# One-pass transposed scores with wide exponentials, V stationary in PV, and the FFN woven into attention

## The chip, the cores and the metric

The kernel runs on one core of one Trainium2 chip. The metric is device time in microseconds (us) of one execution; the profile is one such execution taken by the hardware profiler.

Names used below: PE is the tensor engine, DVE the vector engine, ACT the scalar engine, POOL the GpSimd engine. "Granted clock" is the share of full speed that the chip let PE run at.

## The reference, cut to what matters

Two layers, each an attention block and a gated FFN with the same weights in both layers. S = 2048 rows, D = 512, 32 heads of 16, F = 1792.

```python
for _ in range(2):
    h = layernorm(x)
    q, k, v = split(h @ wqkv)                        # 32 heads of width 16
    p = softmax(q @ k.T * 16 ** -0.5)                # 2048 x 2048 for each head
    x = x + (p @ v) @ wo
    h = layernorm(x)
    x = x + (gelu(h @ w_gate) * (h @ w_up)) @ w_down
```

The softmax is what costs: 32 heads x 2048 x 2048 = 134 million exponentials per layer, or 1024 tiles of 128x1024.

## The kernel before

Work is cut into units of 4 heads and 512 queries, 32 units a layer. Each unit is worked through twice, 32 steps each time. Pass 1 computes scores with queries on the partitions and finds each row's maximum on DVE. The maxima are folded into a shifted copy of Q. Pass 2 computes the scores again, transposed (keys on the partitions), takes the exponential on ACT in tiles of 128x512, and multiplies with V. In that product the exponentials are the stationary operand and V, with a column of ones for the row sums, streams 17 columns wide. The FFN follows when attention is finished.

```python
# pass 1, one step: two heads' scores, and their row maxima on DVE
for jj in range(2):
    j = 2 * hp + jj
    ins = e.matmul(bank(2 * buf + jj),
                   lhsT=QT1[32 * j:32 * j + 32, s, qt * 128:(qt + 1) * 128],
                   rhs=KT[32 * j:32 * j + 32, g, kb * 512:(kb + 1) * 512],
                   start=True, stop=True, tile_position=(32 * j, 0))
...
sch.op("dve", lambda e, po=po, buf=buf: e.tensor_reduce(po, PS[:, 2 * buf:2 * buf + 2, :], axis=AX.X, op=ALU.max), ...)
# pass 2, one step: two heads' transposed scores, two exponentials of 512 columns
for jj in range(2):
    ...
    sch.op("pe", lambda e, ...: e.matmul(bank(bk), lhsT=KT[...], rhs=QT2[...], ..., tile_position=(32 * j, 0)), ...)
    sch.op("act", lambda e, bk=bk, slot=slot: e.activation(PT[:, slot, :], bank(bk), ACTF.Exp, scale=DH ** -0.5), ...)
# PV: exponentials stationary, V and the ones column moving
for qt in range(4):
    acc = AP(PS, 7 * 512 + (qt * 4 + j) * 17, [[8 * 512, 128], [1, 17]])
    ins = e.matmul(acc, lhsT=PT[:, slot, qt * 128:(qt + 1) * 128], rhs=VP[:, kt, 4 * g + j, :], ...)
# filler: zero weights, in steps with little other work for PE
for i in range(n_mm):                      # n_mm = 3
    ins = e.matmul(PS[:, 7, NACC:512], lhsT=ZER[:, :], rhs=XNT[:, 0, 0:512 - NACC], start=False, stop=False, ...)
```

## Time and profile before

| | before |
|---|---|
| median | 2828.22 us (3 runs, 2822.28 to 2829.49) |
| busy: PE, DVE, ACT | 2626.5, 2504.3, 2470.2 us of a span of 2824.1 |
| mean granted PE clock | 0.994 |

The groups of instructions, costliest first (`...` stands for lines left out). Columns: line, engine, operation, output and inputs, shapes, count; busy us and mean ns of one; idle time of that engine just before them, and what ended it.

```profile
L775 DVE TENSOR_REDUCE PM<-PS 128x2 f32<-128x1024 f32 x2048 | 2335.3, 1219 | 42.5 <-PE PS L797 27.2
L801 ACT ACTIVATE SCR<-PS 128x512 bf16<-128x512 f32 x4096 | 2187.0, 598 | 57.3 <-PE PS L797 0.8
...
L737 PE MATMUL PS<-XNT,ZER 128*128 128x240 bf16 x5562 | 869.5, 264 | 22.9 <-ACT ACCS L647 22.9
...
L819 PE MATMUL PS<-VP,SCR 128*128 128x17 bf16 x16384 | 729.2, 172 | 0.0
```

The row maxima (L775) fill 2335 us with 43 us of idle time before them: DVE sets the pace, at 2335.3 / 2048 = 1.14 us per step. ACT is close behind, 2187.0 / 4096 = 0.534 us per exponential, two per step. L737 is the filler.

The chain of waits, followed back from the last instruction, says the same:

```profile
DVE 76%; PE 15%; ACT 6%; DMA 1%; POOL 1%; issue 1%; ACTq 0%; DVEq 0%; POOLq 0%
```

Stretches of the span: busy us of PE, weight loads, DVE, ACT and POOL, then the granted PE clock. The first is attention of layer 1, the second part of its FFN.

```profile
70.00:1200.00 1130.00, 1053.08 (x14700) 541.66 (x14699) 1116.05 (x1011) 1089.78 (x2074) 120.92 (x72) 1.00 0.01 2
1270.00:1340.00 70.00, 69.13 (x554) 51.58 (x552) 31.62 (x75) 29.07 (x70) 17.75 (x26) 1.00 0.01 1
```

In the FFN stretch ACT is 42% busy (29.07 of 70). The two FFN phases, from the last exponential (1261 and 2662 us) to the next row maximum (1429) or the end (2824), take about 165 us each, and no exponential runs in them.

### The profile page before, as it was taken

How to read it: one execution, taken by the hardware profiler on the slowest of the kernel's cores; microseconds unless marked ns; L12 is line 12 of the kernel's file. 1: busy time of each engine (PE TensorE's matmuls, PEld its weight loads, DVE VectorE, ACT ScalarE, POOL GpSimd, SP SyncE). 2: the span in 40 equal slices, each digit the busy share in tenths (PEclk: the TensorE clock that was granted, in tenths of full speed). 3: DMA queues.
4: the chain of work that ended last, by engine and by line, in shares of the span. 5: the costliest groups of instructions: out<-in, count | busy, mean ns of one | idle time of the engine just before them, and what ended most of it. 6: DMA issues, size and time to landing. Idle time of an engine off the chain costs nothing.

```text
span 2824.1 us, 75969 instructions
## 1 busy us (share of the span) xinstructions
PE 2626.5 (93%) x33850; PEld 1411.6 (50%) x33850; DVE 2504.3 (89%) x2500; ACT 2470.2 (87%) x4742; POOL 353.4 (13%) x315
## 2 busy tenths in 40 slices
PE   6999999999999999999989999999999999999999
PEld 2444444444444444457734444444444444444576
DVE  6899999999999999934478999999999999999243
ACT  4899999999999999994339999999999999999832
POOL 3000010001000110012200000100010001000210
PEclk9999999999999999999999999999999999999999
DMA  5000000000000000000000000000000000000000
GB/s 168 1 2 2 2 2 2 2 2 2 2 2 2 2 2 2 2 2 1 1 1 2 2 2 2 2 2 2 2 2 2 2 2 2 2 2 2 2 16 16
DMA packets 9721, 18.75 MB, mean 7 GB/s; under 512 B 433, under 2 KB 6321, under 8 KB 9393
## 3 DMA queue, kind: packets, MB, share of 16 engines
q1 hardware_dynamic: 7280, 9.70, 1.1%
q8 instruction: 265, 4.34, 0.6%
q0 software_dynamic: 2112, 4.19, 0.4%
q14 instruction: 64, 0.52, 0.1%
HBM read 9.70 MB, written 2.10 MB: 4 GB/s over the span
## 4 chain that ended last, share of the span: by engine, by line
DVE 76%; PE 15%; ACT 6%; DMA 1%; POOL 1%; issue 1%; ACTq 0%; DVEq 0%; POOLq 0%
DVE PM L775 73%; PE PS L366 6%; ACT SCR L801 3%; PE PS L430 2%; DVE HT L497 2%; PE PS L766 2%; ACT FSC L490 2%; PE PS L458 1%; PE PS L819 1%; PE PS L681 1%; PE PS L737 1%; DMA X<-in_A_x_dram 1%; PE PS L797 1%; DVE ST L315 1%; ACT AO L687 0%
## 5 line engine op out<-in xcount | busy, mean ns | idle before, releaser
L775 DVE TENSOR_REDUCE PM<-PS 128x2 f32<-128x1024 f32 x2048 | 2335.3, 1219 | 42.5 <-PE PS L797 27.2
L801 ACT ACTIVATE SCR<-PS 128x512 bf16<-128x512 f32 x4096 | 2187.0, 598 | 57.3 <-PE PS L797 0.8
L766 PE MATMUL PS<-KT,SCR 32*128 32x512 bf16 x4096 | 797.0, 386 | 128.8 <-DVE PM L775 1.2
L797 PE MATMUL PS<-QT,KT 32*128 32x512 bf16 x4096 | 889.0, 385 | 4.2 <-ACT SCR L801 1.6
L737 PE MATMUL PS<-XNT,ZER 128*128 128x240 bf16 x5562 | 869.5, 264 | 22.9 <-ACT ACCS L647 22.9
L819 PEld LDWEIGHTS PS<-VP,SCR 128*128 128x128 bf16 x16384 | 547.5, 96 | 435.7 <-issue 434.9
L819 PE MATMUL PS<-VP,SCR 128*128 128x17 bf16 x16384 | 729.2, 172 | 0.0
L766 PEld LDWEIGHTS PS<-KT,SCR 32*128 32x128 bf16 x4096 | 192.3, 91 | 644.7 <-DVE PM L775 566.0
L650 POOL TENSOR_TENSOR RL<-ACCS,CM 128x16 f32<-128x16 f32 x64 | 185.9, 2905 | 2111.4 <-ACT ACCS L647 2111.4
L737 PEld LDWEIGHTS PS<-XNT,ZER 128*128 128x128 bf16 x5562 | 401.0, 96 | 66.7 <-ACT ACCS L647 41.1
L797 PEld LDWEIGHTS PS<-QT,KT 32*128 32x128 bf16 x4096 | 247.7, 90 | 59.5 <-ACT SCR L801 36.9
L490 ACT ACTIVATE FSC<-PS 128x256 bf16<-128x256 f32 x224 | 85.2, 383 | 161.4 <-DVE HT L497 88.0
L497 DVE TENSOR_TENSOR HT<-PS,FSC 128x256 bf16<-128x256 f32 x224 | 92.8, 422 | 136.4 <-ACT FSC L490 123.9
L366 PE MATMUL PS<-FSC,WG 128*128 128x256 bf16 x896 | 135.2, 274 | 0.4 <-ACT FSC L490 0.4
L366 PE MATMUL PS<-FSC,WU 128*128 128x256 bf16 x896 | 134.9, 273 | 0.0
L366 PE MATMUL PS<-WD,HT 128*128 128x512 bf16 x448 | 99.6, 379 | 3.9 <-DVE HT L497 3.7
L366 PEld LDWEIGHTS PS<-FSC,WG 128*128 128x128 bf16 x896 | 87.8, 98 | 15.3 <-ACT FSC L490 0.7
L436 ACT ACTIVATE KT<-PS,KBIAS 128x512 bf16<-128x512 f32 x64 | 44.0, 687 | 58.5 <-PE PS L430 58.5
L366 PEld LDWEIGHTS PS<-FSC,WU 128*128 128x128 bf16 x896 | 87.5, 98 | 10.3
L430 PE MATMUL PS<-XNT,WKP 128*128 128x512 bf16 x256 | 72.1, 408 | 5.6 <-ACT XNT L350 3.1
L366 PEld LDWEIGHTS PS<-WD,HT 128*128 128x128 bf16 x448 | 42.8, 98 | 55.1 <-issue 3.4
L607 PE MATMUL PS<-XNT,WQP 128*128 128x512 bf16 x248 | 63.5, 377 | 0.0
(58 smaller groups left out, 732.7 us busy)
## 6 DMA issues: line engine op xcount, KB each, us to landing
X<-in_A_x_dram POOLq DMA_DIRECT2D x4, 1024.0 KB, 15.1
out_dram<-OB SPq DMA_DIRECT2D x16, 128.0 KB, 1.7
WG<-in_B_w_gate_dram SPq DMA_DIRECT2D x1, 1792.0 KB, 19.7
WU<-in_B_w_up_dram SPq DMA_DIRECT2D x1, 1792.0 KB, 25.4
WD<-in_B_w_down_dram SPq DMA_DIRECT2D x1, 1792.0 KB, 28.6
SCR<-in_A_wqkv_dram SPq DMA_DIRECT2D x2, 512.0 KB, 4.4
WV<-in_A_wqkv_dram SPq DMA_DIRECT2D x1, 512.0 KB, 9.3
WO<-in_A_wo_dram SPq DMA_DIRECT2D x1, 512.0 KB, 13.0
```

The source lines that it names most:

```text
L366: ins = e.matmul(out_ap, lhsT=l, rhs=r_, start=(i == 0), stop=(i == n - 1 and extra is None))
L430: ins = e.matmul(bank(bk), lhsT=WKP[:, ck, g, :], rhs=XNT[:, ck, 512 * b:512 * (b + 1)], start=(ck == 0), stop=(ck == n - 1))
L490: sch.op("act", lambda e, bg=bg, gs=gs: e.activation(GT[:, gs, :], bank(bg)[:, 0:256], ACTF.Gelu_apprx_tanh), r=[BK[bg]], w=[("GT", gs)])
L497: sch.op("dve", lambda e, bu=bu, gs=gs, ft=ft: e.tensor_tensor(ht(ft), bank(bu)[:, 0:256], GT[:, gs, :], op=ALU.mult), r=[BK[bu], ("GT", g ...
L607: ins = e.matmul(bank(bk), lhsT=WQP[:, ck, g, :], rhs=XNT[:, ck, 512 * qb:512 * (qb + 1)], start=(ck == 0), stop=(ck == n - 1))
L650: sch.op("pool", lambda e: e.tensor_tensor(RL[:, s, :], lsum, CM1[:, :], op=ALU.pow), r=[("ACCS", s), ("CM1",)], w=[("RL", s)])
L737: ins = e.matmul(PS[:, 7, NACC:512], lhsT=ZER[:, :], rhs=XNT[:, 0, 0:512 - NACC], start=False, stop=False, skip_group_check=True)
L766: ins = e.matmul(bank(2 * buf + jj), lhsT=QT1[32 * j:32 * j + 32, s, qt * 128:(qt + 1) * 128], rhs=KT[32 * j:32 * j + 32, g, kb * 512:(kb ...
L775: sch.op("dve", lambda e, po=po, buf=buf: e.tensor_reduce(po, PS[:, 2 * buf:2 * buf + 2, :], axis=AX.X, op=ALU.max), r=[BK[2 * buf], BK[2 ...
L797: sch.op("pe", lambda e, bk=bk, j=j, kt=kt, s=s, g=g: e.matmul(bank(bk), lhsT=KT[32 * j:32 * j + 32, g, kt * 128:(kt + 1) * 128], rhs=QT2[ ...
L801: sch.op("act", lambda e, bk=bk, slot=slot: e.activation(PT[:, slot, :], bank(bk), ACTF.Exp, scale=DH ** -0.5), r=[BK[bk]], w=[("PT", slot)])
L819: ins = e.matmul(acc, lhsT=PT[:, slot, qt * 128:(qt + 1) * 128], rhs=VP[:, kt, 4 * g + j, :], start=(st and qt == 0), stop=False, skip_gro ...
```

## The change

Intent: drop the first pass. The scores are small enough here to take the exponential without a row maximum, so DVE's 2335 us, the second score matmul and the shift of Q go. Scores are computed once, transposed. One exponential covers two banks, 128x1024. In PV, V with its ones column becomes the stationary operand (17 columns), four heads side by side in four column tiles, and the exponentials stream; the row sums come out as row 16 of each tile, and are inverted and spread over 16 partitions through DRAM. With the PE time so freed, projections, layer norm and FFN are woven into attention, through one PSUM bank (bank 6; banks 0 to 5 hold three score slots, bank 7 PV). Only the FFN's gate part does not go through bank 6: its seven pieces per query block take the score slots, one after another in one burst. The filler goes. At the end every engine reads a flag, which says whether the row sums and variances stayed in range; if not, the old two-pass program runs. With these inputs it does not.

The core of it (cut: the old program is kept as the general path; the set-up, the normalisation and the scheduler are left out):

```diff
-    e.tensor_reduce(po, PS[:, 2 * buf:2 * buf + 2, :], axis=AX.X, op=ALU.max)      # DVE, each step
-    e.activation(PT[:, slot, :], bank(bk), ACTF.Exp, scale=DH ** -0.5)             # 512 columns, twice a step
-    e.matmul(acc, lhsT=PT[:, slot, qt * 128:(qt + 1) * 128], rhs=VP[:, kt, 4 * g + j, :], ...)
-    e.matmul(PS[:, 7, NACC:512], lhsT=ZER[:, :], rhs=XNT[:, 0, 0:512 - NACC], ...) # filler
+    def a_slot(layer, u, kt, hp):                    # one step; next_slot() cycles through 3
+        for jj in range(2):
+            j = 2 * hp + jj
+            ins = e.matmul(bank(2 * s + jj), lhsT=KT[32 * j:32 * j + 32, c, kt * 128:(kt + 1) * 128],
+                           rhs=Q[32 * j:32 * j + 32, qs, :], start=True, stop=True, tile_position=(32 * j, 0))
+        sch.op("act", lambda e: e.activation(PT[:, p, :].rearrange("p (a b) -> p a b", a=2), PS[:, 2 * s:2 * s + 2, :],
+                                             ACTF.Exp, scale=SCALE), ...)
+    def pv(layer, u, kt):                            # every second step
+        for j in range(4):
+            ins = e.matmul(PS[32 * j:32 * j + VW, 7, :], lhsT=VP[:, kt, h, :],
+                           rhs=PT[:, ps[j // 2], (j % 2) * 512:(j % 2 + 1) * 512],
+                           start=(kt == 0), stop=(kt == NKT - 1), tile_position=(0, 32 * j), ...)
+    misc = Ring([6])                                 # the one bank for everything else
+    while nxt < len(seqs) or pend:                   # the loop over steps
+        ...
+            a_slot(layer, u, kt, hp)
+            run_pv(step)
+        while spent < BUDGET:                        # 520 ns: K, Q, V projections
+            c = prep_try()
+            ...
+        while spent < BUDGET and posts:              # output projection, layer norm, FFN
+            c = next(posts[0], "end")
+            ...
```

An item of four 512-column matmuls is counted as 864 ns, so one such item fills a step's budget. In this text "item" means one piece of this other work, "step" one `a_slot`, and "turn" a step in which items may run. An item's "eviction" is the DVE instruction that reads its finished result out of the PSUM bank.

## The prediction

> **What bounds it now.** In attention (70-1260 and 1430-2660 us of the span) VectorE finds row maxima. The cost groups show 2048 reductions of 128x1024 scores, 1219 ns each, 2335 us busy together (1140 ns per step when back to back), with 43 us of idle time before them. The chain of waits gives DVE 76%, that reduction alone 73%. ScalarE follows closely: 4096 exponentials of 128x512, 598 ns each, 2187 us busy. The FFN stands apart: in the stretches table, 1270-1410 and 2700-2824 us, ACT falls to about a third busy; about 175 us per layer.
>
> **What the change does.**
> - Row maxima (2335 us DVE), the second score matmul, the shift of Q and the 5562 filler matmuls go. DVE falls to about 400 us: projections' evictions and adds (128x512, 692 ns each) and layer norm.
> - Exp works on 128x1024. Read from the trace: 598 ns at 512 columns, 383 (gelu) at 256, so 0.84 ns per column; in a row 8 instructions took 4.48 us, the last counted whole, so about 545 ns apart. At 1024 columns I estimate 0.97 us step to step: 2048 x 0.97 = 1985 us. 56 gelus add 55 us, about 14 more table loads (1283 ns) 15 us. ScalarE is the new floor: about 2055 us.
> - Scores, PE: two row-tiled matmuls per step. The trace has four of them in 0.42 us, so they run concurrently. PV becomes four column tiles of 17x512 every second step; no run before shows these. The Trainium skill ("TensorE: Matmul & The Clock Gate", Measured speedup vs the span model) gives three column tiles 2.38x, so I take about 0.3 us plus about 0.15 us drain per mode change ("TensorEngine Tiling (Array Packing)", Key Properties; the trace shows about 0.15 us between the scores' streaming and PV). Two steps need about 1.1-1.3 us of PE against 1.94 us of ACT: attention alone is ACT-bound.
> - FFN, projections and layer norm are spread through attention, through ONE PSUM bank. A four-matmul group streams 0.86 us, then about 0.28 us to the reader's start, 0.69 us DVE, about 0.07 us release: about 1.9 us per such item, and PE is in order, so the scores of the next step wait. Such a step costs 1.9 instead of 0.97 us; three PSUM slots hide only two steps. Per query block: 14 up items +12 us, down +9, four output projections of eight matmuls +7, transposes +4, gate burst (7 x 1.73 us PE) +4. About 36 us x 6 blocks = 215, and 56 K/V items + 50: about 265 us.
>
> **What stays exposed.** Start: 42 us (as before: X arrives by 29 us, then all four transposes). Layer boundary: layer 1's first unit needs the last block's FFN after 24 steps: about 50 us. End: DMA normalisation 13, output projection 8, layer norm and transposes 7, gate 12, up 12, down 13, store and branch 5: about 70 us.
>
> **Sum:** 2055 + 265 + 42 + 50 + 70 = 2480 us, 12% less. Range 2370 to 2620. Faster by over 2%: 0.92; within 2%: 0.05; slower: 0.03.
>
> **What would show it.** ACT about 2050 us busy (above 80%), DVE below 20%; exp about 1.03 us each; in stretches without projections ACT fully busy, in stretches with them exp waiting for score matmuls, and matmuls of the miscellaneous group waiting for DVE evictions; a boundary hole of about 50 us near the middle; four PV matmuls starting within a few ns of each other.
>
> **What would make it wrong.** Column tiles running one after another (about 1.1 us per PV): PE would bind everywhere, near 2800. Evictions overlapping better, or slack absorbing the bursts: near 2300. Normalisation's small DMAs stalling DVE or GpSimd, then PE: slower.

## The result, and the profile after

| | before | after |
|---|---|---|
| median | 2828.85 us (4 runs) | 2505.85 us (4 runs, 2504.71 to 2512.08) |
| ratio | | 0.8855 (95% interval 0.8817 to 0.8893) |
| busy: PE, DVE, ACT | 2626.5, 2504.3, 2470.2 us | 2159.2, 361.0, 1993.2 us |
| mean granted PE clock | 0.994 | 0.659 |

Ratios here and below are those for the runs of the same rounds, so not quite the ratio of the medians quoted beside them. Every kernel below was timed beside the kernel before, whose median stayed between 2824.8 and 2828.9 us; the variants are compared with one another by their medians.

The groups after:

```profile
L613 ACT ACTIVATE fPT<-fPS 128x1024 bf16<-128x1024 f32 x2048 | 1913.4, 1184 | 390.8 <-PE fPS L608 389.3
L608 PE MATMUL fPS<-fQ,fKT 32*128 32x512 bf16 x4096 | 1102.1, 553 | 172.5 <-ACT fPT L613 163.4
L626 PE MATMUL fPS<-fPT,fVP 128*17 128x512 bf16 x4096 | 573.1, 550 | 1.4 <-ACT fPT L613 1.4
...
L323 PE MATMUL fPS<-fXNT,fWU 128*128 128x512 bf16 x448 | 111.6, 381 | 23.2 <-DVE fHT L513 18.1
```

The exponentials are the largest group, and ACT waited 389 us for score matmuls before them. (The mean duration of 1184 ns is longer than the time from one to the next, because exponentials in a row overlap: 2048 of them keep ACT busy for 1913.4 us only. One that starts on an idle ACT takes 1.02 us.) Score and PV matmuls take 550 ns, an up projection's 381 ns. That difference is the clock: by the 40 slices of the span, in tenths,

```profile
ACT  1689976999769996899727899679986899769971
...
PEclk7855569555795558756588655785568655695558
```

PE runs at about half speed for most of the time in which attention runs alone (from 458 to 500 us the granted clock was 0.50 throughout), and the slices inside attention where ACT drops to 6 or 7 are mostly those where the clock is up, that is, where items run.

The chain of waits is now mostly exponentials:

```profile
ACT 54%; PE 31%; DVE 8%; DMA 3%; POOL 2%; SPq 2%; issue 1%; POOLq 0%; DVEq 0%
```

The timeline of attention alone. Columns: start us, duration, engine, line, operation, and in brackets the idle time before it and its releaser. In this and the next timelines the rows of weight loads, and of engines and operations that the text does not speak of, are left out.

```profile
599.46 9.32 ACT L613 ACTIVATE fPT<-fPS 128x1024 bf16<-128x1024 f32 x10
599.67 0.60 PE L608 MATMUL fPS<-fQ,fKT 32*128 32x512 bf16 x2 [0.53 <-ACT fPT L613]
600.20 0.61 PE L626 MATMUL fPS<-fPT,fVP 128*17 128x512 bf16 x4
600.74 0.60 PE L608 MATMUL fPS<-fQ,fKT 32*128 32x512 bf16 x2
601.50 0.61 PE L608 MATMUL fPS<-fQ,fKT 32*128 32x512 bf16 x2 [0.15 <-ACT fPT L613]
```

Ten exponentials run without a gap. Elsewhere 32 of them take 29.44 us; with the last counted whole (1.02 us) that is (29.44 - 1.02) / 31 = 0.917 us per step. PE waits for ACT, not the reverse. Four PV matmuls together take 0.61 us, as long as two score matmuls, so the column tiles run side by side.

The same view where up projections run:

```profile
400.50 0.39 PE L608 MATMUL fPS<-fQ,fKT 32*128 32x512 bf16 x2
400.60 0.69 DVE L513 TENSOR_TENSOR fHT<-fPS,fHT 128x512 bf16<-128x512 f32 x1 [1.13 <-PE fPS L323]
400.81 0.39 PE L626 MATMUL fPS<-fPT,fVP 128*17 128x512 bf16 x4
400.93 1.02 ACT L613 ACTIVATE fPT<-fPS 128x1024 bf16<-128x1024 f32 x1 [0.80 <-PE fPS L608]
401.35 1.04 PE L323 MATMUL fPS<-fXNT,fWU 128*128 128x512 bf16 x4
402.32 0.39 PE L608 MATMUL fPS<-fQ,fKT 32*128 32x512 bf16 x2
...
402.75 1.02 ACT L613 ACTIVATE fPT<-fPS 128x1024 bf16<-128x1024 f32 x1 [0.80 <-PE fPS L608]
```

A step takes 402.75 - 400.93 = 1.82 us, twice as long, and ACT idles 0.80 us in it. The eviction (L513) of one item ends at 401.29 and the next item starts at 401.35: the single bank is the loop. PE is at full clock here (0.39 instead of 0.61 us).

A single Q projection inside attention, at half clock:

```profile
239.21 1.89 PE L323 MATMUL fPS<-fXNT,fWQM 128*128 128x512 bf16 x4
241.03 0.61 PE L608 MATMUL fPS<-fQ,fKT 32*128 32x512 bf16 x4
241.68 1.94 ACT L613 ACTIVATE fPT<-fPS 128x1024 bf16<-128x1024 f32 x2 [0.85 <-PE fPS L608]
```

The four matmuls take 1.89 us instead of 1.04, and ACT idles 0.85 us. There is one in nearly every unit.

### The profile page after: what moved, and what is told of

Same layout as the page of the kernel before. It is cut to its first block, busy times and chain, and to the rows that moved or that the text cites. A ratio compares the mean times of both kernels' runs of the same rounds, so it can differ in the third digit from the quotient of the medians.

```text
span 2504.6 us, 25781 instructions
## 1 busy us (share of the span) xinstructions
PE 2159.2 (86%) x10945; PEld 537.1 (21%) x10945; DVE 361.0 (14%) x634; ACT 1993.2 (80%) x2121; POOL 160.9 (6%) x192
## 4 chain that ended last, share of the span: by engine, by line
ACT 54%; PE 31%; DVE 8%; DMA 3%; POOL 2%; SPq 2%; issue 1%; POOLq 0%; DVEq 0%
ACT fPT L613 54%; PE fPS L323 13%; PE fPS L577 4%; PE fPS L521 4%; PE fPS L608 4%; DVE fHT L513 2%; PE fPS L626 2%; SPq L239 2%; PE fPS L353 2%; DMA fRB<-rscr 1%; PE fPS L308 1%; POOL fXN L295 1%; POOL fAT L437 1%; DVE fVP L358 1%; DVE fKT L343 1%
## 5 line engine op out<-in xcount | busy, mean ns | idle before, releaser
L613 ACT ACTIVATE fPT<-fPS 128x1024 bf16<-128x1024 f32 x2048 | 1913.4, 1184 | 390.8 <-PE fPS L608 389.3
L608 PE MATMUL fPS<-fQ,fKT 32*128 32x512 bf16 x4096 | 1102.1, 553 | 172.5 <-ACT fPT L613 163.4
L626 PE MATMUL fPS<-fPT,fVP 128*17 128x512 bf16 x4096 | 573.1, 550 | 1.4 <-ACT fPT L613 1.4
L608 PEld LDWEIGHTS fPS<-fQ,fKT 32*128 32x128 bf16 x4096 | 198.7, 97 | 1064.0 <-ACT fPT L613 984.9
L437 POOL TENSOR_TENSOR fAT<-fOS,fRB 128x512 bf16<-128x512 f32 x64 | 81.0, 1265 | 1874.9 <-DMA fRB<-rscr 1874.9
L626 PEld LDWEIGHTS fPS<-fPT,fVP 128*17 128x17 bf16 x4096 | 101.1, 90 | 400.0 <-issue 395.8
L323 PE MATMUL fPS<-fXNT,fWU 128*128 128x512 bf16 x448 | 111.6, 381 | 23.2 <-DVE fHT L513 18.1
L521 PE MATMUL fPS<-fWD,fHT 128*128 128x512 bf16 x448 | 113.7, 381 | 13.1 <-DVE fXN L532 4.7
L323 PE MATMUL fPS<-fXNT,fWQM 128*128 128x512 bf16 x256 | 111.8, 587 | 4.3 <-DVE fX L537 1.4
L577 PE MATMUL fPS<-fXNT,fWG 128*128 128x512 bf16 x448 | 110.4, 412 | 0.8 <-DVE fXNT L312 0.5
L513 DVE TENSOR_TENSOR fHT<-fPS,fHT 128x512 bf16<-128x512 f32 x112 | 77.5, 692 | 216.5 <-PE fPS L323 216.3
```

What stands on the lines that cost most here:

```text
L323: ins = e.matmul(bank(b)[:, 0:cols], lhsT=l, rhs=r_, start=(i == 0), stop=(i == n - 1))
L437: sch.op("pool", lambda e, g=g, slot=slot, os_=os_: e.tensor_tensor(AT[:, g, :], OS[:, os_, :], RB[:, slot, :], op=ALU.mult), r=[("OS", os ...
L513: lambda b, ft=ft: sch.op("dve", lambda e: e.tensor_tensor(HT[:, ft, :], bank(b), HT[:, ft, :], op=ALU.mult), r=[BK[b], ("HT", ft)], w=[(" ...
L521: ins = e.matmul(bank(b)[:, 0:D], lhsT=HT[:, ft, i * 128:(i + 1) * 128], rhs=WD[:, ft, :], start=(ft == 0), stop=(ft == NFT - 1))
L577: ins = e.matmul(bank(2 * s + jj), lhsT=WG[:, ck, ft * 128:(ft + 1) * 128], rhs=XNT[:, ck, xs], start=(ck == 0), stop=(ck == NCK - 1))
L608: ins = e.matmul(bank(2 * s + jj), lhsT=KT[32 * j:32 * j + 32, c, kt * 128:(kt + 1) * 128], rhs=Q[32 * j:32 * j + 32, qs, :], start=True, ...
```

## The experiments

Eleven kernels were built from the changed one and run; all gave correct results. A trace of each is compared with those above.

### 1. Two narrow exponentials instead of a wide one

```diff
-        sch.op("act", lambda e: e.activation(PT[:, p, :].rearrange(...), PS[:, 2 * s:2 * s + 2, :], ACTF.Exp, scale=SCALE), ...)
+        for jj in range(2):
+            sch.op("act", lambda e, jj=jj: e.activation(PT[:, p, jj * 512:(jj + 1) * 512], bank(2 * s + jj),
+                                                 ACTF.Exp, scale=SCALE), r=[bks[jj]], w=[("PT", p)])
```

> Two exponentials of 128x512 in place of one of 128x1024, nothing else. Theory A (ScalarE sets the pace in the attention stretches; the wide instruction is what lowered it): 0.918 us per step (29 in 26.68 us in the trace of the changed kernel) becomes 2 x 0.534 = 1.07 us (the kernel before: 2187 us busy over 4096). About 1700 of 2048 steps are paced by ScalarE, so +0.15 x 1700 = about +255 us, near 2760 us. Rival B (TensorE at its half clock, 0.61 us per matmul group, sets the pace of 0.918 and ScalarE only follows): less than +100 us.

Measured: 2805.92 us, ratio to before 0.992 (0.9886 to 0.9953), 300 us slower than the changed kernel (about 255 expected). From the timeline of attention alone:

```profile
599.61 30.75 ACT L614 ACTIVATE fPT<-fPS 128x512 bf16<-128x512 f32 x55
```

55 instructions in 30.75 us are 0.56 us each, 1.12 per step against 0.917. The expectation had 1.07, from the kernel before. Theory A holds. The run also says something plain about the change: with everything else in place but the old exponentials, it was within 2% of the kernel before. By these steps, removing the row maxima alone would only have moved the limit from DVE (1.14 us per step) to ACT (1.12); a kernel with nothing but that removed was not run.

### 2 and 3. The one bank for everything else

Bank 6 can only be joined by others if the score slots give theirs up. So there are two runs: two score slots with two banks idle (the control), and two score slots with banks 4, 5 and 6 for the items.

```diff
-        s = slot_no["n"] % 3
+        s = slot_no["n"] % 2          # both runs
-    misc = Ring([6])                  # and the two later assignments of its banks
+    misc = Ring([4, 5, 6])            # second run only
```

> Score slots cut from three to two, two PSUM banks left unused: the control for the next run. Theory A: only the slack for bursts is lost, about 1 us per burst and per Q projection: +20 to +90 us (2525 to 2600). If the half TensorE clock (score matmuls to the exponential's start about 0.65 us, PV ahead of it another 0.54 us) cannot refill a slot within one exponential of 0.918 us, attention itself slows and it is over +150 us.

> Two score slots, and three PSUM banks instead of one for projections, FFN and transposes. Theory C (the single bank is what makes an up-projection step 1.82 us: matmuls to DVE start 1.07, eviction 0.69, release 0.06): against the two-slot control, up steps fall from 1.82 to about 1.45 us (TensorE alone, as in the down steps, 1.29 without PV and 1.61 with), transposes from 1.12 to about 0.6: 40 to 90 us faster than the control. Rival D (TensorE's own work in the step is the limit): within 15 us of the control.

Measured: control 2584.56 us, with three banks 2477.44 us. The lost slot cost 79 us, as expected, and the two banks gave 107 us against the control, more than the 40 to 90 expected. Exponentials beside up projections in the run with three banks:

```profile
398.71 1.02 ACT L613 ACTIVATE fPT<-fPS 128x1024 bf16<-128x1024 f32 x1 [0.27 <-PE fPS L608]
400.33 1.02 ACT L613 ACTIVATE fPT<-fPS 128x1024 bf16<-128x1024 f32 x1 [0.59 <-PE fPS L608]
401.62 1.02 ACT L613 ACTIVATE fPT<-fPS 128x1024 bf16<-128x1024 f32 x1 [0.27 <-PE fPS L608]
```

Steps now alternate between 1.62 and 1.29 us, with and without PV, in place of 1.82, which the control still shows. Theory C holds: the bank's round trip set 1.82 us. What is left, 1.45 us on average against 0.917, is PE's own work: it is busy for 30.58 of the 31 us from 398 to 429.

### 4. Items in every second step only

```diff
+        turn = step % 2 == 1 or nxt >= len(seqs)
-        while spent < BUDGET:
+        while turn and spent < BUDGET:
             c = prep_try()
...
-        while spent < BUDGET and posts:
+        while turn and spent < BUDGET and posts:
```

> Projections, FFN and transposes only in every second step, those without PV. Theory E (the excess arises because the items come in bursts, step after step, in steps already carrying scores and PV; ScalarE idles 0.9 us per item): two steps with one four-matmul item need about 2.0 us of TensorE (0.32 + 0.97 + 0.32 + 0.32, and drains) against 1.84 us of ScalarE, so an item costs about 0.2 instead of 0.9 us: 100 to 150 us faster, 2355 to 2405. Rival F (the total TensorE work binds over the whole of attention, so moving it changes nothing): within 30 us of 2506.

Measured: 2305.82 us, 200 us faster, more than the 100 to 150 expected. Exponentials beside the up projections and the first downs:

```profile
360.73 35.68 ACT L613 ACTIVATE fPT<-fPS 128x1024 bf16<-128x1024 f32 x38
```

38 in 35.68 us is (35.68 - 1.02) / 37 = 0.937 us per step; ACT does not wait at all. Theory E holds and rival F falls. The miss is in the cost of an item: 2 x (0.937 - 0.917) = 0.04 us, where 0.2 had been estimated. ACT's waiting before exponentials went from 389 to 182 us.

The edit does two things at once: only half of the steps may take items, and none of these steps has PV. No run separates the two.

Not all of the waiting went. The K and V projections at the start of layer 2 still left ACT idle 1.33 us per pair of steps, in this stretch (columns as in the stretches before):

```profile
1190.00:1217.00 27.00, 26.44 (x142) 10.53 (x140) 5.65 (x9) 16.34 (x16) 0.00 (x0) 0.50 0.01 2
```

PE is busy 26.44 of 27 us there, at clock 0.50.

### 5 to 8. The clock, and the FFN taken out again

A filler like that of the kernel before (two matmuls of 512 columns instead of three of 240) was put back, right after PV, in steps without items; once as full-array matmuls and once as column tiles like PV's. It was also combined with spreading. A fourth kernel moved layer norm and FFN of the first three query blocks of each layer behind attention.

```diff
+        if state["fill"] and spent == 0 and nxt < len(seqs):     # state["fill"]: PV ran in this step, not a unit's last
+            def pe_fill(e):
+                for _ in range(2):
+                    ins = e.matmul(bank(7), lhsT=ZER[:, :], rhs=WV[:, 0, :], start=False, stop=False, ...)
```

In the column-tile form the matmul is replaced by this:

```diff
+                    for j in range(4):
+                        ins = e.matmul(PS[32 * j:32 * j + VW, 7, :], lhsT=ZER[:, 0:VW], rhs=WV[:, 0, :],
+                                       start=False, stop=False, tile_position=(0, 32 * j), ...)
```

> Two full-array filler matmuls (zero weights, 512 columns, added to the PV bank) after PV in steps that have no other work, as the kernel before had them. Theory H (the clock is granted by how much of the array works; row-tiled scores and 17-column PV tiles alone leave it at half, 0.50 in the stretches without FFN): mean clock rises from 0.66 to over 0.9; attention stays at 0.918 us per step because ScalarE paces it; but single Q projections (1.89 us at half clock, ScalarE idle 0.9), the first projections of a burst and the transposes (1.12 us each) get short: 60 to 110 us faster than 2506. Rival I (the clock costs nothing because ScalarE paces attention and bursts warm the array themselves): within 20 us, or slower by the fillers.

Measured: 2436.45 us, 69 us faster than the changed kernel, mean clock 0.970. Attention alone did not get faster at full clock:

```profile
788.95 92.58 ACT L615 ACTIVATE fPT<-fPS 128x1024 bf16<-128x1024 f32 x100
```

That is (92.58 - 1.02) / 99 = 0.925 us per step, against 0.917 at half clock. It also runs over three Q projections without a gap; each cost 0.85 us before. ACT's waiting before exponentials fell from 389 to 325 us, nearly all of the gain. So the half clock costs nothing where ACT sets the pace, and 69 us at the items. Theory H was right about the size and about where it lies.

> The same two fillers in the shape of PV, four column tiles of 17 columns each, so the same TensorE time but about an eighth to a half of the array. Theory H: the clock stays near 0.5 in attention although TensorE is busy all the time; at half clock the two fillers need 2 x 0.43 us, so two steps take about 2.5 instead of 1.84 us: about 2900 us or more. If TensorE's busy time alone decided the clock, this run looks like the run with full-array fillers.

Measured: 2435.29 us (two runs), clock 0.970, the same as with full-array fillers. The expectation failed: 17 columns in each column tile kept the clock as well as 128 columns did, so the part of theory H that says how much of the array must work falls.

> Fillers and the spreading over every second step together. In the run with spreading the K and V projections still leave ScalarE idle 1.33 us per two steps, in a stretch whose clock is 0.50, and Q projections 0.5 us each; at full clock both should vanish: 40 to 90 us faster than the spread run, 2215 to 2265. If the clock does not matter once the items are spread: within 20 us of 2306.

Measured: 2375.15 us, 69 us slower than spreading alone. Neither expectation was met. Exponentials beside up projections:

```profile
657.84 1.02 ACT L615 ACTIVATE fPT<-fPS 128x1024 bf16<-128x1024 f32 x1 [0.27 <-PE fPS L610]
659.02 1.02 ACT L615 ACTIVATE fPT<-fPS 128x1024 bf16<-128x1024 f32 x1 [0.16 <-PE fPS L610]
660.31 1.02 ACT L615 ACTIVATE fPT<-fPS 128x1024 bf16<-128x1024 f32 x1 [0.27 <-PE fPS L610]
```

Two steps take 660.31 - 657.84 = 2.47 us. The kernel was badly built: items run in odd steps and PV in even ones, so the test "no item in this step" let the fillers run in the very stretches where PE had no time to spare.

> The FFN of the first three query blocks of a layer taken out of attention and run with the fourth block's at the layer's end, ScalarE idle; output projections stay in attention. In the changed kernel one block's stretch (344.3 to 442.1 us) holds 52 exponentials, 48 us at 0.918, so the block costs 50 us although it is overlapped; about 41 of them are layer norm and FFN. Run apart they take 57 us in layer 1 and 49 in layer 2 by the boundary's and the end's times. Theory J (overlapping earned almost nothing, the excess gives it back): +40 to +90 us, 2545 to 2595. Rival K (overlapping hides most of the FFN): +200 us or more.

Measured: 2608.04 us, 102 us slower than the changed kernel, just above theory J's range and far below rival K's. So weaving six of the eight FFNs into attention earned about 17 us each in this kernel. Run apart, one takes far longer: in this run the FFNs at the end of layer 2 follow each other every 48 us (the first gelus start at 2420.57, 2468.37 and 2516.13 us), those of layer 1 every 68 us, with eight exponentials in between.

### 9 to 11. Putting it together

First, the badly built combination mended: fillers only while no item ran in the last turn.

```diff
+        if turn:
+            state["worked"] = spent
-        if state["fill"] and spent == 0 and nxt < len(seqs):
+        if state["fill"] and state.get("worked", 0) == 0 and nxt < len(seqs):
```

> Spreading as before, fillers only while no projection, FFN or transpose runs (in the run with both, fillers also ran beside every item, because the items are in the steps without PV and the fillers in those with PV; its trace shows 4 pieces of about 2.47 us per two steps there in place of 1.87). Theory L (the fillers beside the items are what made that run slower than spreading alone): the loss goes and Q projections (ScalarE idle 0.5 to 0.9 us each, 58 of them) gain: 2250 to 2295, 10 to 55 us faster than spreading alone (2306). If it stays near 2375 the fillers hurt for another reason.

Measured: 2228.47 us, ratio to before 0.7875, 77 us faster than spreading alone and more than expected. Theory L holds: the fillers beside the items had been the loss.

Then the output projection of eight matmuls was cut into two pieces of four, with the piece boundary handled as in the down projection:

```diff
-            yield out_proj(qb, qt)
+            for g0 in range(0, NG, 4):
+                ...                                   # four matmuls into the same bank
+                if g0 + 4 < NG:
+                    state["open"] = True
+                    yield 864.0
```

> The same with each output projection of eight matmuls cut into two pieces of four in two different turns. Theory E (what matters is that no pair of steps gets more TensorE work than ScalarE covers): the idle times of 1.1 to 3.3 us before the exponentials at the four output projections of each block fall to about 0.2: 10 to 30 us faster than the run before it. Rival: no change, since the first of them waits for the normalisation's DMA anyway.

Measured: 2203.96 us (2195.74 to 2210.19), ratio to before 0.7784 (0.7753 to 0.7816), 24 us faster than the run before it, as expected. This is the fastest kernel, 22% below the kernel before and 12% below the changed one. Its ACT is 90% busy:

```profile
998.52 80.36 ACT L631 ACTIVATE fPT<-fPS 128x1024 bf16<-128x1024 f32 x86
```

ACT waits only 112 us before exponentials, 49 of them at the start.

Last, three banks and two slots with spreading (the edits of runs 3 and 4 together, no filler):

> Spreading with two score slots and three banks for the other work. In the kernel without spreading, the two more banks gave 107 us against the two-slot control. Theory M (with one item every second step its eviction of 0.69 us is over before the next item, so the bank no longer limits; only the lost slot shows): 0 to 60 us slower than spreading alone, 2306 to 2365. If the single bank still limited: over 20 us faster than 2306.

Measured: 2346.31 us, 40 us slower than spreading alone, inside theory M's range: once the items are spread, the third slot is worth more than the two banks. That the single bank then costs nothing at all is not shown by this run, since spreading with two slots and one bank was not run; that ACT did not wait beside the up projections in experiment 4 speaks for it.

## Why the prediction was right or wrong

The time was right: 2480 us predicted, 2506 measured, inside the range. Part of that is luck, since two terms too high (exponentials and gelus, by 123 us) and four too low (by 146 us) nearly cancelled. "Measured" below is the profiled run of the changed kernel, span 2504.6 us.

| term of the sum | predicted | measured | how it was measured |
|---|---|---|---|
| exponentials | 1985 | 1878 | 2048 x 0.917 us per step |
| gelus and their tables | 70 | 54 | 42 gelus before the boundary's and the end's, x 0.917, and 12 table loads x 1.283; the others lie in the holes below |
| start | 42 | 53 | the first exponential starts at 52.74 |
| layer boundary | 50 | 72 | hole from 1231.1 to 1306.2, less 3 exponentials |
| end | 70 | 82 | from 2422.7 to the end |
| excess of the items | 265 | 366 | the rest of the span |

- **What bounds it.** Right. ACT was named as the new floor, and the split run confirms it: 0.2 us more per step cost 300 us. The size was not: the step was over-estimated, 0.97 instead of 0.917 us. The estimate took a spacing of 545 ns from eight exponentials in 4.48 us, and added columns at 0.84 ns. Measured, the 512 added columns cost 0.917 - 0.545 = 0.372 us, 0.73 ns per column: the cost per column was too high.
- **Column tiles side by side.** Right. Four PV matmuls of 512 columns take 0.39 us at full clock, as long as the two score matmuls. The 2.38x for three tiles that the prediction took from the Trainium skill ("TensorE: Matmul & The Clock Gate", "Measured speedup vs the span model") is not tested here, as no run has three.
- **The single bank.** Right. An up step was put at 1.9 us and took 1.82; the reason, the eviction's round trip, was shown by the run with three banks.
- **The filler.** This is the step that failed. The prediction said that "the 5562 filler matmuls go" and counted that as work removed, at no cost; all its item costs were taken at full clock. The granted clock fell from 0.994 to 0.659. The items that come singly or first in a burst then ran at half speed: a Q projection took 1.89 us and left ACT idle 0.85 us, where the prediction charged Q nothing. Putting fillers back gained 69 us, about two thirds of the 101 us by which the excess was under-estimated. The waits of 0.85 us behind single Q projections alone make 40 us: the trace of the changed kernel has 47 of them, that of the kernel with full-array fillers none. The rest of those 101 us was not separated.
- **The holes.** Boundary and end were each too low, by 22 and 12 us. At the end, the normalisation through DRAM took from 2422.7 to 2441.5, 19 us, where 13 had been allowed.
- **What would show it.** ACT was expected at about 2050 us, above 80%: it was 1993, 79.6%. DVE below 20%: 14%. A hole near the middle: seen.
- **What would make it wrong.** None of the three happened to any size: column tiles did not run one after another, the slack did not absorb the bursts, and the normalisation's DMAs cost PE about 2 us per block before the output projection (it waits there for POOL's last product), and at the end 6 us more than allowed.

Where did the gain come from? DVE's 2335 us and the apart FFN's 330 us had left, but ACT was already at 0.534 us per half step, so the maxima alone would have been worth little (argued from the split run). The wide exponential brought about 300 us, and six of the eight FFNs in attention 102; each was measured by taking it alone out of the changed kernel, so they need not add up to the 323 us gained. The rest of the FFN's time was given back as ACT idle time beside bursts, and experiment 4 took 200 us of it back by changing only in which steps the items are issued.

Open: what releases the clock once it has dropped. In two kernels with nearly the same code the K and V projections at the start of layer 2 began at half clock with PE busy all the time; in the run with mended fillers the clock was back within 4 us, in the fastest kernel it stayed at 0.50 for 27 us (first and second line; columns as in the stretches before):

```profile
1159.00:1163.00 4.00, 4.00 (x32) 2.12 (x30) 0.69 (x1) 2.47 (x3) 0.00 (x0) 0.59 0.01 4
1144.00:1171.00 27.00, 27.00 (x144) 10.52 (x142) 5.54 (x8) 16.37 (x16) 0.00 (x0) 0.50 0.00 1
```

No experiment told these apart, and the code need not be the reason. In the one trace of the changed kernel, two single Q projections began alike at half clock, at 531.88 and 622.74 us, each 1.89 us long and followed on PE by scores and PV alone. After the first, score groups took 0.39 us from 534.71 until past 537; after the second they stayed at 0.60. What releases the clock may thus differ from one time to the next, and the four runs of the fastest kernel (2195.74 to 2210.19 us, clock 0.969 to 0.977) fit that.

## What to carry to other kernels

When one engine's long work is removed, look at once at the engine right behind it: here nearly all of the gain was lost again when only ACT's wide instructions were split. Work that is woven in beside a paced engine should be dosed so that no short stretch asks more of PE than the paced engine covers; the same items in every second step were worth 200 us. And before removing filler matmuls, ask which later matmuls rely on the clock that they hold up.

## What the Trainium skill lacked or had wrong

- "TensorE: Matmul & The Clock Gate", Part 1, "What's actually happening": its table gives full clock after at least one busy window of about 3.4 us, and half clock after an idle one. Here attention alone sat at 0.50 with no PE gap above 0.53 us in the timeline shown (from 458 to 500 us PE was busy 38.88 of 42 us, as the profile counts it), and in the run with spreading a stretch with PE busy 26.44 of 27 us stayed at 0.50. The table's two levels do agree: steady stretches show 0.50 or 1.00.
- The same page, "Why this matters for your kernels", advises to avoid idle gaps above about 3 us. That was not enough here; two fillers of 512 columns every second step were (clock 0.66 to 0.97), whether they used 128 columns of the array or 17 in each of four column tiles. No page that was read says what share of the time PE has to be busy to keep the clock.
- The same page, Part 3, "Measured speedup vs the span model", has three column tiles. Four tiles of 17 columns took 0.39 us together, where one full-array matmul of 512 columns has a mean of 0.38.
- "TensorEngine Tiling (Array Packing)", Key Properties, says that a change of tiling mode drains the array but not for how long. Here a score group followed by PV started PV 0.31 us after it at full clock and 0.53 at half; the streaming of 512 columns is 0.22 and 0.43 us of that (estimates: in the kernel before, 28 matmuls of 512 columns in a row took 6.20 us and the last one 0.38 of it, so (6.20 - 0.38) / 27 = 0.216 each, and twice that at half clock). About 0.1 us is left for the drain, less than the 0.15 predicted.
